# Other experts for the block ahead, the f32 form and the last group, with loads put ahead of the gathers and statistics behind

## The chip, the cores and the metric

The kernel runs on one core of a Trainium2 chip. The core has five engines that work side by side, each through its own list of instructions in order: TensorE (PE, matrix products), VectorE (DVE), ScalarE (ACT), GpSimd (POOL) and SyncE (SP, which here issues transfers). They meet by semaphores: an instruction may wait until another engine has counted something off, and all behind it on its engine wait too. The metric is the time of one execution in microseconds (us), median of several runs.

## The reference

```python
x = attention(q, k, v)                      # 4 batches, 8 heads, 576 tokens, 64 wide, causal by blocks of 64
x = elu(x @ w_in) @ w_out                   # 2304 tokens, 512 -> 2048 -> 512
do_compute = x @ w_skip > 0                 # the other tokens stay as they are
xc = x[do_compute]
e_idx = argmax(xc @ w_gate)                 # one of 8 experts for each token
gate_w = softmax(xc @ w_gate)[e_idx]
for e in range(8):                          # w1: 512 -> 1024, w2: 1024 -> 512
    y[e_idx == e] = gate_w * (relu(xc[e_idx == e] @ w1[e]) @ w2[e])
out[do_compute] = xc + y
```

With the inputs that are timed, experts 0 to 7 get 176, 2, 5, 91, 283, 192, 453 and 14 tokens.

## The kernel before

Attention, the dense layers and the choice of experts take the first 600 us or so. They are one stream of recorded instructions: `Recorder` notes each instruction with an estimated duration and what it reads and writes, and `order` puts them into a list for each engine. It goes by the earliest time at which an instruction can start by these estimates (`ready` sets a floor for it), takes steps marked `urgent` first, and lets other steps in where they end before the next urgent one would start. The lists are fixed when the kernel is built.

The experts follow. **Preparing an expert.** Its weights come in eight pieces of 512 KB (`load_w`), four for w1 (half 0) and four for w2 (half 1). For each half a statistic of every piece is taken (`stat_w`: the sum of squares on ACT, named jk, or the largest magnitude on DVE), a scale is worked out from it (`scale_w`, with a one-column matmul ns on PE), and each piece is then split into two f16 parts (`split_p`: one part by ACT, the other by DVE). A product of two f32 numbers becomes three f16 products. Experts in `PLAIN` aren't prepared: their blocks multiply in f32.

**A block** (`block`) works on 128 tokens, or on 64 where it is the first of an expert in `SMALL`. The tokens are gathered by POOL (an indirect transfer into gp) and transposed by a transfer that SP issues, into mxt or mxwo. PE makes hp in four groups of 24 matmuls; for each group ACT takes the relu (r) and the f16 part of it (hh), DVE the rest of it (hh); PE makes y from these; ACT scales y into o; POOL scatters o, added to the output. An f32 block has one record of PE for each pass over the weights, 64 for hp and 32 for y with 64 tokens.

**Order of the experts.** Blocks in `AHEAD` run before the counts of all experts are known, amid the end of the routing (their tiles are ahp, hha and ya). Then the experts in `ORDER` follow. Each has a first block in straight code (`first_tokens`) and then nested branches, one for each further 128 tokens (`more_tokens`); the innermost that isn't taken leads back to common code. Expert 2 has no straight block here, only the branches. Each of these places is scheduled by itself. The four experts of `LAST` have one straight stretch of four blocks, and a branch for further tokens.

**What is prepared beside what** stands in `PREP`: "6:l5-1 l3-0 c4-1 p4-1 s5-0|s5-1 c5-0 p5-0|..." means that beside expert 6's first block half 1 of expert 5 and half 0 of 3 are loaded (l), half 1 of 4 gets its scale (c) and is split (p) and half 0 of 5 gets its statistics (s); beside its next block what stands after the bar. `split_beside` records these steps behind the block's own; loads get the floor 5.0 us, statistics 2.0. A loaded piece needs a free place; a split gives the raw piece's place back. If a branch isn't taken, its share of the preparation stands in the other arm.

In what follows 6.0 is the first block of expert 6 behind the blocks ahead, 6.1 the next one. The blocks that run in this kernel are: ahead, expert 0 with 128 and expert 2 with 64 tokens; 6.0 to 6.3 with 128; 4.0 with 64, 4.1 and 4.2 with 128; 5.0 with 64, 5.1 with 128; and in the last group 0 with 64, 3 with 128, 1 and 7 with 64 in f32.

Of the kernel before, what the change touches and what calls it, by code (L numbers as in the profile page):

```python
# [24 lines left out]
PLAIN = 1, 7  # L25
EARLY = 0, 2, 6

SMALL = 0, 1, 4, 5, 7
# [319 lines left out]
def tile_kernel(ctx, tc, q, k, v, w_in, w_out, w_skip, w_gate, w1, w2, out):  # L348
# [34 lines left out]
    pm = const.tile([128, 4], F32)  # L383
# [40 lines left out]
    def setup_consts():  # L424
# [8 lines left out]
        for e in (2,) + SMALL:  # L433
            nc.vector.memset(carry[:, e:e + 1], 64.0)
        nc.gpsimd.iota(pm[:, 2:3], pattern=[[0, 1]], base=64, channel_multiplier=1, allow_small_or_imprecise_dtypes=True)
# [633 lines left out]
    AHEAD = [(0, 128), (2, 64)]  # L1069
    AH = {}  # L1070

    def ahead_gather():
# [13 lines left out]
        for i, (e, T) in enumerate(AHEAD):  # L1086
# [3 lines left out]
            rank = pm[:, 2:3] if T == 128 else pm[:, 0:1]  # L1090
            rc.gpsimd.tensor_scalar(out=a[:, 2:3], in0=rank, scalar1=carry[:, e:e + 1], scalar2=2 * BIG, op0=ALU.is_ge, op1=ALU.mult)

            rc.gpsimd.tensor_scalar(out=carry[:, e:e + 1], in0=carry[:, e:e + 1], scalar1=64.0 + T, scalar2=None, op0=ALU.max)
# [375 lines left out]
    def scale_w(e, which):  # L1469
# [11 lines left out]
        rc.tensor.matmul(out=p2, lhsT=ones16, rhs=cb, start=True, stop=True)  # L1481
        rc.vector.tensor_copy(acc[:, 5:6], p2)
# [16 lines left out]
    def prep_steps(e, which):  # L1499
        P_ = functools.partial  # L1500
        return ([("stat", P_(stat_w, e, which, x)) for x in range(4)] + [("scale", P_(scale_w, e, which))]
                + [("split", P_(split_p, e, 4 * which + x)) for x in range(4)])
# [22 lines left out]
    load_half(4, 0)  # L1525
    load_half(4, 1)
# [16 lines left out]
    io = mo.tile([128, 8 * NS], F32, tag="g", bufs=GB, name="io")  # L1543
# [46 lines left out]
    def fac_w(e):  # L1590
# [105 lines left out]
    def pre_gather(e):  # L1696
# [11 lines left out]
    def split_beside(e, part, at=5.0):  # L1708
        for h in sum(aside_of(e, part), []):
            if h[0] == "l":  # L1710
                load_half(int(h[1]), int(h[3]), at)
                continue
            for kind, f in prep_steps(int(h[1]), int(h[3])):
                if kind[1] == {"s": "t", "c": "c", "p": "p"}[h[0]]:
# [3 lines left out]
                    if h[0] == "s":  # L1718
                        rc.ready[len(rc.steps) - 1] = 2.0
# [10 lines left out]
    def first_tokens(e, fs):  # L1730
# [3 lines left out]
        rc.urgent = True  # L1734
        tokens(e, 0, place_of(e, 0), fs)
# [6 lines left out]
    def last_tokens(fs):  # L1742
# [19 lines left out]
    def more_tokens(e, j, fs):  # L1762
# [4 lines left out]
        with tc.If(cnt[e] > 128 * j, preferred_fallthrough_block=True, label=f"n{e}_{j}") as cmp:  # L1767
            if j < TM // 128:
# [4 lines left out]
                for x in {0: (0, 1, 2), 1: (1, 2, 3) if e in LAST else (3,)}.get(j, ()):  # L1773
# [42 lines left out]
    pre_gather(ORDER[1])  # L1816
# [57 lines left out]
    for h in "s4-0 s4-1 c4-0 p4-0 l5-0".split():  # L1874
# [8 lines left out]
    pre_gather(ORDER[2])  # L1883
# [43 lines left out]
```

## Time and profile before

| | us |
|---|---|
| median of three runs | 784.36 |
| lowest, highest | 783.33, 787.3 |
| the profiled execution | 785.88 |
| its span, first to last instruction | 784.0 |
| PE busy | 700.9 (89%) |
| DVE busy | 570.4 (73%) |
| ACT busy | 511.3 (65%) |

Times in the trace count from the start of the span; what the profiled execution took beyond it is 1.88 us. A busy share is an average over the whole span, in which the stages differ. For a list that is fixed, the question at each place is which engine stands, and what released it. The rows below are in the stretch from 600 us to the end. In a timeline row a bracket says how long the engine had been idle before, and what ended that; "ACTq" is ACT's sequencer, the part that handles branches and counts, and "PEld" is the loading of weights.

### The profile page before, as it was taken

What the parts mean: (1) busy time and instruction counts of PE and PEld (TensorE: products, weight loads), DVE (VectorE), ACT (ScalarE), POOL (GpSimd) and SP (SyncE); (2) the same over time, 40 slices, a digit from 0 to 9 for tenths busy, and PEclk for the clock granted to TensorE, in tenths of its full rate; (3) what the DMA queues carried; (4) which work ended last, traced back from release to release, by engine and by line L of the source; (5) the groups of instructions that cost most, each with busy time, mean ns of one, the idle gap of its engine ahead of it and who ended that gap; (6) DMA issues with size and microseconds to landing.
All of it is one profiled execution on the core that took longest, in us unless ns stands there. A gap on an engine that the chain in (4) does not pass through costs nothing. (4 is left out here: it accounts for less than half of the span.)

```text
span 784.0 us, 18160 instructions
## 1 busy us (share of the span) xinstructions
PE 700.9 (89%) x6766; PEld 466.2 (59%) x6766; DVE 570.4 (73%) x1710; ACT 511.3 (65%) x1132; POOL 92.0 (12%) x182
## 2 busy tenths in 40 slices
PE   4689997999998999989999999999999779869894
PEld 2467534764465655556656667675766656637673
DVE  5987999788997987978689648997777637143200
ACT  5966558989986886877587537673666667544310
POOL 2000000110001100101000100101040431313211
PEclk8579999999999999999999999999999898979998
DMA  9999899886979899999186189271546794492960
GB/s 263 298 257 281 258 255 199 168 134 125 183 146 139 146 197 180 157 184 179 38 145 125 32 173 382 74 224 42 182 106 185 151 269 109 80 273 46 292 158 5
DMA packets 279742, 134.03 MB, mean 171 GB/s; under 512 B 249291, under 2 KB 258005, under 8 KB 279120
## 3 DMA queue, kind: packets, MB, share of 16 engines
q1 hardware_dynamic: 275520, 125.42, 70.4%
q0 software_dynamic: 4112, 7.23, 4.6%
q8 instruction: 58, 0.95, 0.5%
q14 instruction: 52, 0.43, 0.2%
HBM read 74.12 MB, written 12.75 MB: 111 GB/s over the span
## 5 line engine op out<-in xcount | busy, mean ns | idle before, releaser
L310 PE MATMUL h<-xt,win 128*128 128x256 f16 x1344 | 158.1, 273 | 1.0 <-DVE n L310 1.0
L310 PE MATMUL y<-wout,g 128*128 128x512 f16 x672 | 157.4, 382 | 0.2 <-DVE g L310 0.2
L310 PEld LDWEIGHTS <-win 128*128 128x128 f16 x1344 | 127.6, 98 | 25.4 <-issue 3.1
L310 PEld LDWEIGHTS <-g 128*128 128x128 f16 x672 | 62.7, 98 | 70.8 <-issue 4.5
L310 ACT ACTIVATE ehl<-e,su 128x64 f16<-128x64 f32 (+4 forms) x208 | 85.7, 470 | 17.6 <-DMA et<-ehl 5.5
L310 ACT ACTIVATE e<-s,mx 128x64 f32<-128x64 f32 (+7 forms) x160 | 78.4, 493 | 25.3 <-DVE mx L310 10.5
L310 DVE SCALAR_TENSOR_TENSOR ehl<-e,su,ehl 128x64 f16<-128x64 f32 (+4 forms) x208 | 84.8, 441 | 6.9 <-ACT ehl L310 6.7
L310 DVE TENSOR_REDUCE mx<-s 128x1 f32<-128x64 f32 (+7 forms) x160 | 70.6, 449 | 13.5 <-PE s L310 12.8
L310 PE MATMUL s<-kt,qt 128*64 128x512 f16 (+7 forms) x640 | 62.8, 305 | 8.4 <-ACT e L310 5.5
L310 PE MATMUL xps<-et,vt 128*64 128x128 f16 (+1 forms) x1440 | 50.4, 219 | 16.2 <-DMA et<-ehl 9.9
L310 PEld LDWEIGHTS <-vt 128*64 128x64 f16 x1440 | 42.0, 115 | 35.5 <-issue 20.1
L310 PE MATMUL h<-xt,twi 128*128 128x256 f32 x256 | 62.1, 394 | 1.1 <-DVE g L310 1.1
L310 PE MATMUL y<-two,g 128*128 128x512 f32 x128 | 61.1, 610 | 0.0
L310 POOL MEMSET ehl<- 128x128 f16 x80 | 16.6, 213 | 357.4 <-DMA et<-ehl 275.6
L310 ACT ACTIVATE el<-h,col 128x512 f32<-128x512 f32 x56 | 38.2, 683 | 29.4 <-PE h L310 28.8
L310 PEld LDWEIGHTS h<-xt,twi 128*128 128x128 f32 x256 | 48.2, 195 | 10.9 <-DVE g L310 1.9
L310 PEld LDWEIGHTS <-qt 128*64 128x64 f16 x640 | 28.1, 114 | 43.2 <-issue 33.7
L310 PE MATMUL y<-p,hh 128*128 128x512 f16 (+1 forms) x222 | 41.0, 359 | 13.1 <-ACT hh L310 11.3
L310 ACT ACTIVATE g<-el,col 128x512 f16<-128x512 f32 x56 | 40.2, 717 | 18.9 <-DVE el L310 17.9
L310 PEld LDWEIGHTS <-hh 128*128 128x128 f16 (+1 forms) x336 | 26.4, 106 | 41.7 <-ACT hh L310 14.3
L1496 DVE SCALAR_TENSOR_TENSOR p<-p,n,p 128x1024 f16<-128x1024 f32 x30 | 38.3, 1281 | 12.3 <-ACT p L1495 12.2
L310 DVE TENSOR_TENSOR hh<-r,hh 128x256 f16<-128x256 f32 x38 | 15.9, 423 | 41.0 <-ACT hh L310 41.0
(231 smaller groups left out, 1185.5 us busy)
## 6 DMA issues: line engine op xcount, KB each, us to landing
p<-in_moe_w_dram SPq DMA_DIRECT2D x46, 512.0 KB, 7.1
rw<-in_moe_w_in_dram SPq DMA_DIRECT2D x16, 512.0 KB, 6.7
rw<-in_moe_w_out_dram SPq DMA_DIRECT2D x16, 512.0 KB, 5.0
pb<-in_moe_w_dram SPq DMA_DIRECT2D x13, 512.0 KB, 3.6
vflat<-in_v_dram SPq DMA_DIRECT2D x4, 1152.0 KB, 7.3
out_dram<-pay SPq DMA_DIRECT2D x18, 256.0 KB, 2.5
pay_d<-pay SPq DMA_DIRECT2D x18, 256.0 KB, 2.9
raw<-in_k_dram SPq DMA_DIRECT2D x16, 256.0 KB
```

The costliest lines, as they stand in the source:

```text
L310: rec.call(e, time, lambda: getattr(self.real, op)(*args, **kw), reads, writes, dma)
L1496: rc.call("dve", 1.2, lambda: nc.vector.scalar_tensor_tensor(out=half(1), in0=raw.t, scalar=sc, in1=half(0), op0=ALU.mult, op1=ALU.subtrac ...
```

## The change

Experts get other parts. The f32 form goes to expert 3 (128 tokens) instead of 1 and 7. The experts that are prepared ahead of everything are 0, 6 and 4 (before 0, 2 and 6). The second block ahead takes 128 tokens of expert 6 instead of 64 of expert 2. Expert 0's rest goes into `ORDER`, where its first block is straight code; expert 2 moves into `LAST`, and has blocks of 64 tokens as the first. Seven experts are prepared in place of six.

The steps beside the blocks get another order. Loads marked l are recorded ahead of the block and of its gathers, without a floor (`load_beside`); those marked m behind, as before. A statistic has the floor 4.0 instead of 2.0 and the scale's matmul the floor 3.0. `PREP` gives each block another share. In `last_tokens` the factors that combine two scales are recorded too, and loads and splits of expert 7 stand beside its blocks. The iota that the routing needs moves into another place in memory.

The blocks that then run are: ahead, 0 and 6 with 128 each; 0.0 with 64; 6.0 to 6.2 with 128; 4 and 5 as before; and in the last group 1 and 2 with 64, 3 with 128 in f32, 7 with 64.

```diff
-PLAIN = 1, 7
-EARLY = 0, 2, 6
-
-SMALL = 0, 1, 4, 5, 7
+PLAIN = 3,
+EARLY = 0, 6, 4
+
+SMALL = 0, 1, 2, 4, 5, 7
...
-    AHEAD = [(0, 128), (2, 64)]
+    AHEAD = [(0, 128), (6, 128)]
...
-            if T == 128:
+            if T == 128 and e not in SMALL:
+                rc.sync.dma_start(out=a[:, 0:2], in_=src[:, 0, :])
...
-    def scale_w(e, which):
+    def scale_w(e, which, wait=0.0):
...
+        if wait:
+            rc.ready[len(rc.steps) - 1] = wait
...
-    load_half(4, 0)
-    load_half(4, 1)
+    load_half(5, 0)
+    load_half(5, 1)
...
-    ORDER = [2, 6, 4, 5]
-    LAST = [0, 3, 1, 7]
-    XP = {2: 0, 6: 1, 4: 2, 5: 0}
+    ORDER = [0, 6, 4, 5]
+    LAST = [1, 2, 3, 7]
+    XP = {0: 1, 6: 2, 4: 0, 5: 1}
...
-    GATHERS = {6: [(6, 2), (5, 0), (5, 1)], 4: [(4, 2), (0, 0), (3, 0)], 5: [(5, 2), (1, 0), (7, 0)]}
+    GATHERS = {0: [], 6: [(6, 2), (4, 0), (4, 1)], 4: [(4, 2), (5, 0), (5, 1), (1, 0), (2, 0)], 5: [(5, 2), (3, 0), (7, 0)]}
...
     PREP = {int(e): [x.split() for x in h.split("|")] for e, h in (y.split(":") for y in (
-        "6:l5-1 l3-0 c4-1 p4-1 s5-0|s5-1 c5-0 p5-0|c5-1 p5-1,4:l3-1 l1-0 s3-0|c3-0 p3-0 s3-1,5:l1-1 l7-0 c3-1 p3-1,7:l7-1").split(","))}
+        "6:l1-1 m2-0 c5-0 p5-0|c5-1 p5-1 s1-0|s1-1 c1-0 p1-0,4:l2-1 m7-0|c1-1 p1-1 s2-0|s2-1 c2-0 p2-0,"
+        "5:l7-1 m3-0 c2-1 p2-1|s7-0 s7-1,8:l3-1 c7-0 p7-0 c7-1 p7-1").split(","))}
...
-    def split_beside(e, part, at=5.0):
+    def load_beside(e, part):
         for h in sum(aside_of(e, part), []):
             if h[0] == "l":
-                load_half(int(h[1]), int(h[3]), at)
+                load_half(int(h[1]), int(h[3]))
+
+    def split_beside(e, part):
+        for h in sum(aside_of(e, part), []):
+            if h[0] == "m":
+                load_half(int(h[1]), int(h[3]), 5.0)
+            if h[0] in "lm":
                 continue
-            for kind, f in prep_steps(int(h[1]), int(h[3])):
+            for kind, f in prep_steps(int(h[1]), int(h[3]), 3.0):
...
-                        rc.ready[len(rc.steps) - 1] = 2.0
+                        rc.ready[len(rc.steps) - 1] = 4.0
...
+        load_beside(e, 0)
         tokens(e, 0, place_of(e, 0), fs)
...
-    def last_tokens(fs):
+    def last_tokens():
 
         rc.begin()
         rc.late = rc.left
-        split_beside(LAST[-1], 0, 0.0)
+        load_beside(8, 0)
+        split_beside(8, 0)
         rc.urgent = True
+        fs = {e: fac_w(e) for e in LAST}
...
-    pre_gather(ORDER[1])
+    gather_to(0, 0)
+    pre_gather(6)
...
-    for h in "s4-0 s4-1 c4-0 p4-0 l5-0".split():
+    for h in "s5-0 s5-1 l1-0".split():
...
-            if e != 2:
+            if i:
                 hint(e, 1, cnt[e])
-                first_tokens(e, fs)
+            first_tokens(e, fs)
+            if i:
                 read_count(ORDER[i + 1] if i + 1 < len(ORDER) else "last")
             n0 = ng[0]
-            more_tokens(e, 0 if e == 2 else 1, fs)
+            more_tokens(e, 1, fs)
             ng[0] = n0
             FREE.extend(WHL.pop(8 * e + x) for x in range(8))
-        fs = {e: fac_w(e) for e in LAST}
         tc.mark_branch_hint_location("last", cnt["last"] > 128, engines=[mybir.EngineType.PE])```

SP's list from the start of expert 4's straight block, of before (the mx tiles are transposed tokens, p, pb and pd places for weights):

```order
L310 DMA_TRANSPOSE mxwo_1509<-gp_1505 128x8x128
L310 DMA_TRANSPOSE mxt_1507<-gp_1506 128x8x128
L310 DMA_TRANSPOSE mxt_1507<-gp_1505 128x8x128
L1450 DMA p_1475<-in_moe_w_dram 128x2x512
L1450 DMA p_7513<-in_moe_w_dram 128x2x512
L1450 DMA p_7528<-in_moe_w_dram 128x2x512
L1450 DMA p_7520<-in_moe_w_dram 128x2x512
L1447 DMA p_7521<-in_moe_w_dram 128x1024
```

and of after:

```order
L1453 DMA pd_1498<-in_moe_w_dram 128x2x512
L1453 DMA pd_1499<-in_moe_w_dram 128x2x512
L1453 DMA p_1476<-in_moe_w_dram 128x2x512
L1453 DMA p_7512<-in_moe_w_dram 128x2x512
L310 DMA_TRANSPOSE mxwo_1509<-gp_1501 128x8x128
L310 DMA_TRANSPOSE mxt_1507<-gp_1501 128x8x128
L310 DMA_TRANSPOSE mxt_1507<-gp_1502 128x8x128
L1450 DMA p_7513<-in_moe_w_dram 128x1024
L1450 DMA p_7514<-in_moe_w_dram 128x1024
```

Four loads stand ahead of the transposes now, and four behind; before all eight stood behind.

ACT's list in block 4.1 of before, from the relu of the first group of hp (jk is a statistic, p is a place being split):

```order
L310 ACTIVATE r_11455<-hp 128x256
L310 ACTIVATE hh<-r_11455 128x256
L1465 ACTIVATE jk,n_88<-p_1475 128x1024
L310 ACTIVATE r_11458<-hp 128x256
L1495 ACTIVATE p_7525<-p_7514,n_88 128x1024
L310 ACTIVATE hh<-r_11458 128x256
L310 ACTIVATE r_11461<-hp 128x256
L1495 ACTIVATE p_7526<-p_7515,n_88 128x1024
L310 ACTIVATE hh<-r_11461 128x256
```

and ACT's list at the end of block 4.2 of after, the last block of expert 4 that runs:

```order
L1468 ACTIVATE jk,n_87<-pd_1498 128x1024
L310 ACTIVATE r_11608<-hp 128x256
L310 ACTIVATE r_11611<-hp 128x256
L310 ACTIVATE hh<-r_11608 128x256
L310 ACTIVATE hh<-r_11611 128x256
L1468 ACTIVATE jk,n_87<-pd_1499 128x1024
L1500 ACTIVATE p_7528<-p_7530,n_87 128x1024
L1500 ACTIVATE p_7529<-p_7531,n_87 128x1024
L310 ACTIVATE o_1510<-y_11600,lists 128x512
L1500 ACTIVATE p_7530<-p_7532,n_87 128x1024
L1500 ACTIVATE p_7531<-p_7533,n_87 128x1024
L1782 COMPARE_AND_BRANCH
```

In before the statistic reads p_1475, the first of the loads that stand behind the transposes in the straight block of the same expert, and three groups of hh stand behind it; block 4.2 has no preparation at all. In after the statistic in 4.2 reads pd_1498, the first load in SP's list of after, and two splits stand between o and the branch.

## Rows read from the trace of the kernel before

**Rows 1.** The page's head, and its dense f32 groups (busy us, mean ns).
```profile
span 784.0 us, 18160 instructions
...
L310 PE MATMUL h<-xt,twi 128*128 128x256 f32 x256 | 62.1, 394 | 1.1 <-DVE g L310 1.1
L310 PE MATMUL y<-two,g 128*128 128x512 f32 x128 | 61.1, 610 | 0.0
```

**Rows 2.** PE's waits, 560 to 784: who is waited for, total, times, longest.
```profile
PE y L310 <- ACT hh L310: 12.6, 4, 7.1
PE hp L310 <- ACTq L1767: 5.7, 4, 3.0
PE ns L310 <- DVE cb L310: 2.0, 2, 1.1
```

**Rows 3.** PE's timeline: start, duration, tile, count, idle time before.
```profile
615.79 0.79 PE L310 MATMUL lp<-mv 128*128 128x152 f32 x4
619.55 1.79 PE L310 MATMUL hp<-mxt,p 128*128 128x128 f16 x24 [2.98 <-ACTq L1767]
622.48 0.16 PE L310 MATMUL ns<-cb,ones 128*128 128x1 bf16 x1 [1.14 <-DVE cb L310]
...
628.86 5.34 PE L310 MATMUL y<-p,hh 128*128 128x512 f16 x24
...
643.39 1.76 PE L310 MATMUL y<-p,hh 128*128 128x512 f16 x6 [2.79 <-ACT hh L310]
...
663.54 5.52 PE L310 MATMUL hp<-mxwo,p 128*128 128x128 f16 x96
668.90 5.34 PE L310 MATMUL y<-p,hh 128*128 128x512 f16 x24
...
696.53 1.03 PE L310 MATMUL y<-p,hh 128*128 128x512 f16 x2 [7.14 <-ACT hh L310]
...
715.21 0.33 PE L310 MATMUL hp<-mxt,pb 128*128 128x64 f16 x6 [0.89 <-ACTq L1767]
...
721.17 0.51 PE L310 MATMUL hp<-mxt,pb 128*128 128x128 f16 x6
...
734.12 4.44 PE L310 MATMUL hp<-mxt,p 128*128 128x64 f16 x120 [0.90 <-ACTq L1767]
...
752.02 7.25 PE L310 MATMUL hp<-x,p 128*128 128x64 f32 x64
```

**Rows 4.** ACT's timeline: splits before the branch, a statistic, the last o.
```profile
617.28 2.17 ACT L1495 ACTIVATE pd<-pb,n 128x1024 f16<-128x1024 f32 x2
...
693.72 1.06 ACT L1465 ACTIVATE jk<-p 128x1024 bf16<-128x1024 f32 x1 [8.62 <-DMA p<-in_moe_w_dram]
...
773.87 0.47 ACT L310 ACTIVATE o<-y,gp 128x256 f32<-128x256 f32 x1 [3.28 <-PEq L1753]
```

**Rows 5.** SP's timeline at expert 4: the first loads.
```profile
688.80 2.15 SPq L1450 DMA_DIRECT2D p<-in_moe_w_dram  x4
```

**Rows 6.** By window: busy PE, PEld, DVE, ACT, POOL, then PEclk, DMA share, GB/s.
```profile
621.00:627.00 6.00, 4.86 (x48) 4.70 (x46) 2.43 (x13) 3.56 (x7) 0.00 (x0) 0.50 0.69 112
...
693.00:702.00 9.00, 5.15 (x12) 1.62 (x13) 5.79 (x7) 8.06 (x14) 0.00 (x0) 0.50 1.04 398
702.00:774.00 72.00, 67.69 (x848) 53.40 (x846) 17.21 (x41) 22.28 (x48) 15.87 (x11) 1.00 0.56 140
```

**Rows 7.** Groups by line and shape, 600 to 784: busy us, mean ns.
```profile
L310 ACT ACTIVATE r<-hp 128x256 f32<-128x256 f32 x42 | 15.8, 379 | 33.9 <-PE hp L310 30.2 <-DVE pd L1496 2.0 <-remote 0.7
L310 ACT ACTIVATE hh<-r 128x256 f16<-128x256 f32 x38 | 15.5, 412 | 0.7
...
L1465 ACT ACTIVATE jk<-p 128x1024 bf16<-128x1024 f32 x8 | 8.4, 1051 | 10.5 <-DMA p<-in_moe_w_dram 10.4
...
L1496 DVE SCALAR_TENSOR_TENSOR p<-p,n,p 128x1024 f16<-128x1024 f32 x6 | 7.7, 1282 | 10.7 <-ACT p L1495 10.6
...
L1495 ACT ACTIVATE p<-p,n 128x1024 f16<-128x1024 f32 x6 | 6.9, 1144 | 0.3 <-DVE pb L1496 0.3
```

More of the change, by code (lines that the diff above doesn't have):

```diff
@@ L432, in setup_consts @@
         nc.vector.memset(carry, 0.0)
-        for e in (2,) + SMALL:
+        for e in SMALL:
             nc.vector.memset(carry[:, e:e + 1], 64.0)
+        nc.gpsimd.iota(pm[:, 4:5], pattern=[[0, 1]], base=0, channel_multiplier=1, allow_small_or_imprecise_dtypes=True)
         nc.gpsimd.iota(pm[:, 2:3], pattern=[[0, 1]], base=64, channel_multiplier=1, allow_small_or_imprecise_dtypes=True)
@@ L1089, in ahead_gather @@
             gp = gp2[:, 512 * i:512 * i + 512]
[L1090 removed]
+            rank = pm[:, 0:1] if T == 64 else pm[:, 2:3] if e in SMALL else pm[:, 4:5]
             rc.gpsimd.tensor_scalar(out=a[:, 2:3], in0=rank, scalar1=carry[:, e:e + 1], scalar2=2 * BIG, op0=ALU.is_ge, op1=ALU.mult)
[L1093 removed]
+            rc.gpsimd.tensor_scalar(out=carry[:, e:e + 1], in0=carry[:, e:e + 1], scalar1=64.0 * (e in SMALL) + T, scalar2=None, op0=ALU.max)
             rc.gpsimd.tensor_scalar(out=ai[:, 3:4], in0=a[:, 0:1], scalar1=2048.0, scalar2=float((AC + 1) * CT - 1), op0=ALU.add, op1=ALU.min)
@@ L1497, in split_p, with prep_steps @@
                 [raw.key, sc, hl.key], [hl.key])
-    def prep_steps(e, which):
+    def prep_steps(e, which, wait=0.0):
         P_ = functools.partial
-        return ([("stat", P_(stat_w, e, which, x)) for x in range(4)] + [("scale", P_(scale_w, e, which))]
+        return ([("stat", P_(stat_w, e, which, x)) for x in range(4)] + [("scale", P_(scale_w, e, which, wait))]
                 + [("split", P_(split_p, e, 4 * which + x)) for x in range(4)])
@@ L1542, in tile_kernel @@
     sl = part(NS)
-    io = mo.tile([128, 8 * NS], F32, tag="g", bufs=GB, name="io")
+    GP = []
+    for i in range(2):
+        t = wp.tile([128, 2, PW], F32, tag=f"wo{i + 4}", bufs=1, name=f"gp{i}")
+        GP += [t[:, 0, :], t[:, 1, :]]
+    more = GP.pop()
+    io = more[:, 352:352 + 8 * NS]
     rc.sync.dma_start(out=lst, in_=lst_d.rearrange("(e p s) w -> p e s w", e=E, p=128))
@@ L1596, in fac_w @@
         hs = half[:, e, C0[e], 1:2]
-        nc.vector.tensor_tensor(out=f, in0=nrm[e][:, 0, 7:8], in1=nrm[e][:, 1, 7:8], op=ALU.mult)
-        nc.vector.tensor_scalar(out=fs, in0=fs, scalar1=f, scalar2=2.0 ** 20, op0=ALU.mult, op1=ALU.mult)
+        rc.vector.tensor_tensor(out=f, in0=nrm[e][:, 0, 7:8], in1=nrm[e][:, 1, 7:8], op=ALU.mult)
+        rc.vector.tensor_scalar(out=fs, in0=fs, scalar1=f, scalar2=2.0 ** 20, op0=ALU.mult, op1=ALU.mult)
         if e in SMALL:
-            nc.vector.tensor_scalar(out=hs, in0=hs, scalar1=f, scalar2=2.0 ** 20, op0=ALU.mult, op1=ALU.mult)
+            rc.vector.tensor_scalar(out=hs, in0=hs, scalar1=f, scalar2=2.0 ** 20, op0=ALU.mult, op1=ALU.mult)
         return fs
@@ L1772, in more_tokens @@
                 rc.urgent = True
-                for x in {0: (0, 1, 2), 1: (1, 2, 3) if e in LAST else (3,)}.get(j, ()):
+                for x in ((1, 2, 3) if e in LAST or e == 0 else (3,)) if j == 1 else ():
                     gather_to(e, x)
```

15 lines of the change are left out of this document (5 added, 10 removed).

## The prediction, made before the changed kernel ran

> **What bounds the kernel now.** I read the page's head first, for the span and the busy shares, then PE's waits from 560 us on, then PE's timeline there, and at each wait the timeline of the engine that ended it. The order of PE is the same up to 600 us; only the experts' stretch behind it is changed, so all that follows is there.
>
> PE is busy for most of that stretch, and where it stands, ACT ended it: 12.6 us in four waits of y for hh, 5.7 us in four waits for ACT's sequencer at branches, 2.0 us in two waits of ns for the scale [rows 2]. The largest, 7.14 us at 696.53 [rows 3], isn't ACT being slow. ACT stood 8.62 us before a statistic at 693.72, and a transfer ended that [rows 4]: the load had been issued at 688.80 only [rows 5], behind three transposes in SP's list, and the groups of hh that y needs stand behind the statistic in ACT's list. The wait of 2.79 us at 643.39 is of the same kind (its statistic stood before a load too). The wait of 2.98 us before 619.55 is another kind: PE's last matmul ended at 616.6 (615.79 + 0.79), ACT's last split at 617.28 + 2.17 = 619.45, and PE goes on 0.1 us later [rows 3, 4]. PE waits at a branch until ACT has done its whole list of that place. Three other such places cost (5.7 - 3.0) / 3 = 0.9 us each [rows 2].
>
> Each long stall has a second price. The granted clock is 0.50, the lower of the two levels (1.2 GHz), from 621 to 627 and from 693 to 702, behind the stalls of 2.98 and 7.14 us, and 1.00 from 702 to 774 although PE stood 0.9 us there twice [rows 3, 6]. From 619.55 to 628.86 the 96 matmuls hp and one wait of 1.14 us took 9.31 us; 96 at the higher clock take 668.90 - 663.54 = 5.36 [rows 3]. So the low clock cost 9.31 - 5.36 - 1.14 = 2.8 us.
>
> **The sum, part by part.** I follow PE, the engine that the end hangs on, and build its new timeline from blocks. A clean block of 128 tokens takes 10.7 us (663.54 to 668.90 + 5.34), one of 64 tokens 721.17 - 715.21 = 6.0 us [rows 3].
>
> *The blocks ahead.* 128 tokens of expert 6 instead of 64 of expert 2: 10.7 - 6.0 = 4.7 us more. PE ended at 616.6 here, so now at 621.3; a little earlier if the longer list fills gaps of the routing. The branch of the empty expert 2, with its 2.98 us, goes, since expert 0's block follows in straight code. Block 0.0 (6.0) and an ordinary branch (0.9): 628.2.
>
> *Expert 6* has three blocks instead of four, which removes 10.7 us. Two costs are new. The statistics and scale of one half and the splits of another now stand beside each of 6.1 and 6.2, where before the last block was clean. ACT's work in 6.1 is four r (0.38), four hh (0.41), four statistics (1.05, with the read-out of the sum about 1.2), four splits (1.14) and o (about 0.7) [rows 7]: 3.2 + 4.8 + 4.6 + 0.7 = 13.3 us against PE's 10.7. So ACT runs late into 6.2, the scale of 6.2 is late, and ns waits; I take 0.8, by the two waits of ns that sum to 2.0 [rows 2]. And behind o two splits still stand before the branch, as the order of 4.2 shows too. The stall of 2.98 us had just this form, o and two splits; with one wait for DVE's part of a split (1.28, [rows 7]) it would be 4.3. I take 3.5, between 0.9 (ACT gets done in time) and 4.3. Expert 6: 3 x 10.7 + 0.8 + 3.5 = 36.4, to 664.6.
>
> *Expert 4* is 4.0, 4.1, 4.2 as before. Removed are the wait of 7.14 us in 4.1 and one of about 1.3 in 4.0 (12.6 less 7.14 and 2.79 leaves 2.7 for two): the pieces whose statistics stand in 4.1 are now loaded beside 6.0, and those of 4.2 by the four loads at the head of SP's list in 4.0. New are the same two costs as at expert 6, and in 4.0 both r stand ahead of both hh, which makes the first hh one r late (with a wait about 0.7). 6.0 + 0.7 + 10.7 + 10.7 + 0.8 + 3.5 = 32.4, to 697.0.
>
> *Expert 5.* Its block 5.1 has eight statistics, the last ones behind o: I take 2.3 us at the branch, two of them, between 0.9 and 3.5. 6.0 + 0.7 + 10.7 + 2.3 = 19.7, to 716.7.
>
> *The last group* took 773.87 - 734.12 = 39.7 us [rows 3, 4]. Now it has three blocks of 64 in f16, 18.0 us, and 128 tokens of expert 3 in f32. The trace has no such block. Its 64 records of hp cost 7.25 us with 64 columns [rows 3], the lower end, and 64 x 62.1 / 256 = 15.5 with 256 columns [rows 1], the upper. Half of the price at 256 columns for half the columns is 7.8, close to the lower end; I take that. Its y has 16 records of 512 columns, 16 x 61.1 / 128 = 7.6 [rows 1]. 18.0 + 7.8 + 7.6 = 33.4, to 750.1. Beside it stand eight splits of expert 7 on ACT (9.2 us) and DVE (10.2), in 27 us before they are needed, and four loads that are due 20 us later: nothing.
>
> The Trainium skill bears on that f32 price. Its page "TensorE: Matmul & The Clock Gate", section "Weight-path perf modes — Fast Weight Load (FWL) and DoubleRow", says that the fast way to load weights is not used for FP32, so that at few columns the loading sets the price. By that rule hp would stay near 7.25, by half of the row of 256 columns it is 7.8; no run here has yet shown 128.
>
> *The end.* From PE's last work to the end of the span is 784.0 - 773.9 = 10.1 us, the last scatter, unchanged: 760.2.
>
> *The clock.* The two stalls of 3.5 us are longer than the 2.98 and 2.79 that had low clock behind them. Twice 2.8: 765.8. The seventh expert's preparation (eight more splits and statistics) is what fills ACT in these places and is priced there; it isn't added again.
>
> On this the Trainium skill (same page, "Loop structure matters more than you think") says that a long wait between bursts of matmuls lets the array fall to the lower clock, which speaks against putting work behind o. The rows at 619.55 and 696.53 agree. By that rule both exits are paid twice; without it the sum would be 5.6 us lower.
>
> The profiled execution took 785.88 with a span of 784.0, so 1.88 lies around it, and it is 1.52 above the median of 784.36. A span of 765.8 gives 765.8 + 1.88 - 1.52 = 766.2. I say 766.
>
> **Rivals.**
>
> *The exits are short.* ACT has finished by PE's end at all three branches (0.9 each instead of 3.5, 3.5 and 2.3, 6.6 less) and the clock stays at 1.00 (5.6 less): 754. For it: ACT is idle in long pieces in 4.2 and 6.3 of before, and lists by estimates can fit. Against: the order puts the splits behind o. Chance 0.14.
>
> *A statistic still waits for a load.* If a load finds no free place in time (the first places of 4.0 come free by splits in 6.2, which are late), one stall like 7.14 with its clock returns: 766 + 7.1 + 2.8 = 776. For it: the loads at 4.0 and 5.0 are only a block or two ahead. Against: before, the load was issued in the very block in which the statistic stood, and 5 us passed from 688.80 to 693.72 [rows 4, 5]; now a block of 6 us at least lies between. Chance 0.14.
>
> *The loads hold back the transposes* (the other side). At 0.0, 4.0, 5.0 and the last group four loads of 512 KB now stand before the transposes; at the 398 GB/s of 693 to 702 [rows 6] 2.1 MB take 5.3 us. If transposes come that late to a block, PE stands 5.3 us and pays 2.8 for the clock, 8.1 a place. With three such places it is 766 + 24 = 790, slower; with two it is 782. For it: SP works in order. Against: what is gathered at 4.0 is used in 4.2 and by expert 5, at least 16 us later. Chance 0.03.
>
> *The change doesn't gain what it moves.* The seventh expert's preparation takes ACT six statistics and eight splits more, 6 x 1.05 + 8 x 1.14 = 15.4 us [rows 7]. If ACT bounded all of the stretch, that would come on top: 781, about no change. Against: ACT stood 10.4 us for transfers before statistics of p places alone [rows 7], time that it can now work in. Chance 0.06.
>
> **How the numbers follow.** The forecast has 0.63 and by itself reaches from 761 (one exit short, clock kept there) to 773 (hp in f32 at the upper end). With the first two rivals 754 to 778 holds 0.85 or somewhat more. What a measurement of this kernel can tell from no change is 0.5%, 3.9 us: faster is below 780.4, slower above 788.3. Faster: 0.63 + 0.14 + 0.14 = 0.91. About the same: 0.05, nearly all of the last rival. Slower: 0.04, the transposes and a part of the last rival.
>
> **What would show it.** Right: no wait of y for hh above 1.5 us behind a statistic that a transfer released; PE's first hp of block 0.0 near 621; waits for ACT's sequencer of some 3.5 us at the ends of 6.2 and 4.2 with the granted clock at 0.50 behind them; the f32 block of expert 3 near 15 us. Wrong: a statistic that still stands for a transfer (the second rival), branches of 0.9 us (the first), waits of hp for a transfer of mxwo or mxt (the third), or PE standing for hh in block after block (the fourth).

## The result, and the profile after

The changed kernel takes 759.03 us (median of four runs, 756.81 to 760.74), the kernel before 785.36 on the same occasions. The ratio is 0.966, with a 95% interval of 0.963 to 0.970. The forecast was 766, with 754 to 778 as its range. The profiled execution took 760.74 with a span of 758.9. Executions that took over 1.5% more than the fastest of their kernel are left out of the ratios below (one each in experiments 2, 3 and 5), and in 2 and 3 it is the profiled one.

PE's waits from 560 us on, of the changed kernel (who is waited for: total, times, longest), answer to [rows 2]:

```profile
PE hp L310 <- ACTq L1782: 9.5, 4, 3.2
PE y L310 <- ACT hh L310: 1.7, 2, 0.8
PE hp L310 <- issue: 1.4, 2, 0.7
PE ns L310 <- DVE cb L310: 0.4, 2, 0.2
```

The waits of y for hh are down from 12.6 us to 1.7, and the waits at branches are up from 5.7 to 9.5. PE's timeline shows where these are (start, duration, what, count, and idle time before it with what ended it):

```profile
616.77 0.68 PE L310 MATMUL lp<-mv 128*128 128x152 f32 x4
617.29 2.96 PE L310 MATMUL hp<-mxt,p 128*128 128x64 f16 x96
620.18 2.81 PE L310 MATMUL y<-p,hh 128*64 128x256 f16 x48
624.14 4.19 PE L310 MATMUL hp<-mxwo,p 128*128 128x128 f16 x72 [1.14 <-ACTq L1782]
...
659.55 4.51 PE L310 MATMUL hp<-mxt,p 128*128 128x64 f16 x96 [3.20 <-ACTq L1782]
664.89 3.05 PE L310 MATMUL y<-p,hh 128*64 128x256 f16 x48 [0.83 <-ACT hh L310]
...
692.74 0.42 PE L310 MATMUL hp<-mxt,p 128*128 128x64 f16 x9 [3.20 <-ACTq L1782]
...
714.48 0.42 PE L310 MATMUL hp<-mxwo,pb 128*128 128x64 f16 x9 [1.97 <-ACTq L1782]
...
728.75 7.41 PE L310 MATMUL hp<-x,p 128*128 128x128 f32 x64
736.00 7.03 PE L310 MATMUL y<-p,r 128*128 128x512 f32 x16
```

From 624.14 to the end of the last y of expert 6, 3.20 us before 659.55, PE never stands longer than 0.2 us, through three blocks. Expert 0's block follows the routing (616.77 + 0.68) at once. The three long waits are at the branches that end experts 6, 4 and 5; I call them exits. ACT's timeline at the first of these, with o and the two splits behind it, and one statistic of 4.1:

```profile
656.40 0.69 ACT L310 ACTIVATE o<-y,lists 128x512 f32<-128x512 f32 x1 [0.72 <-PE y L310]
656.98 1.14 ACT L1500 ACTIVATE pb<-pd,n 128x1024 f16<-128x1024 f32 x1
658.31 1.15 ACT L1500 ACTIVATE pd<-pd,n 128x1024 f16<-128x1024 f32 x1 [0.19 <-DVE pb L1501]
...
672.39 1.05 ACT L1468 ACTIVATE jk<-p 128x1024 bf16<-128x1024 f32 x1
```

The last split ends at 659.46 and PE goes on at 659.55. The statistic at 672.39 has no idle time before it; the one in the same block before stood 8.62 us for its load [rows 4]. In the windows behind the exits (busy PE, PEld, DVE, ACT, POOL, then the granted clock, the transfers' share and GB/s) the clock is near the lower level, as in [rows 6]:

```profile
660.00:664.00 4.00, 4.00 (x87) 3.94 (x83) 1.29 (x4) 0.39 (x1) 0.00 (x0) 0.57 0.74 139
664.00:668.00 4.00, 3.12 (x53) 2.59 (x51) 1.45 (x6) 1.00 (x4) 3.11 (x3) 1.00 0.85 243
...
694.50:698.00 3.50, 3.44 (x64) 3.35 (x63) 1.02 (x7) 0.38 (x1) 0.00 (x0) 0.53 1.18 262
...
714.50:718.00 3.50, 3.50 (x72) 3.50 (x72) 0.90 (x8) 0.80 (x2) 0.71 (x1) 0.55 0.93 284
```

### The profile page after: what moved, and what is told of

The parts are those of the page before. It is cut to its first block, busy times and chain, and to the rows that moved or that the text cites. A ratio compares the mean times of both kernels' runs of the same rounds, so it can differ in the third digit from the quotient of the medians.

```text
span 758.9 us, 18318 instructions
## 1 busy us (share of the span) xinstructions
PE 686.4 (90%) x6824; PEld 461.8 (61%) x6824; DVE 583.2 (77%) x1736; ACT 523.8 (69%) x1148; POOL 98.9 (13%) x183
## 5 line engine op out<-in xcount | busy, mean ns | idle before, releaser
L310 PE MATMUL h<-xt,win 128*128 128x256 f16 x1344 | 158.1, 273 | 1.0 <-DVE n L310 1.0
L310 PE MATMUL y<-wout,g 128*128 128x512 f16 x672 | 156.0, 380 | 0.0
L310 PEld LDWEIGHTS <-win 128*128 128x128 f16 x1344 | 127.6, 98 | 25.4 <-issue 3.1
L310 PEld LDWEIGHTS <-g 128*128 128x128 f16 x672 | 62.5, 98 | 69.7 <-issue 3.4
L310 ACT ACTIVATE ehl<-e,su 128x64 f16<-128x64 f32 (+4 forms) x208 | 85.7, 471 | 17.2 <-DMA et<-ehl 5.5
L310 ACT ACTIVATE e<-s,mx 128x64 f32<-128x64 f32 (+7 forms) x160 | 78.6, 494 | 24.3 <-DVE mx L310 10.8
L310 DVE SCALAR_TENSOR_TENSOR ehl<-e,su,ehl 128x64 f16<-128x64 f32 (+4 forms) x208 | 84.8, 440 | 5.7 <-ACT ehl L310 5.4
L310 DVE TENSOR_REDUCE mx<-s 128x1 f32<-128x64 f32 (+7 forms) x160 | 70.5, 448 | 14.8 <-PE s L310 14.2
L310 PE MATMUL s<-kt,qt 128*64 128x512 f16 (+7 forms) x640 | 62.9, 306 | 7.6 <-ACT e L310 4.1
L310 PE MATMUL h<-xt,twi 128*128 128x256 f32 x256 | 62.8, 396 | 1.4 <-DVE g L310 1.3
L310 PE MATMUL xps<-et,vt 128*64 128x128 f16 (+1 forms) x1440 | 50.5, 219 | 14.7 <-DMA et<-ehl 6.7
L310 POOL MEMSET ehl<- 128x128 f16 x80 | 16.8, 216 | 356.8 <-DMA et<-ehl 248.2
L310 PEld LDWEIGHTS <-vt 128*64 128x64 f16 x1440 | 42.1, 115 | 34.1 <-issue 20.0
L310 PE MATMUL y<-two,g 128*128 128x512 f32 x128 | 60.9, 609 | 0.0
L310 ACT ACTIVATE el<-h,col 128x512 f32<-128x512 f32 x56 | 38.3, 683 | 28.6 <-PE h L310 28.0
L310 PEld LDWEIGHTS h<-xt,twi 128*128 128x128 f32 x256 | 48.4, 195 | 11.6 <-DVE g L310 2.6
L310 PEld LDWEIGHTS <-p 128*128 128x128 f16 x936 | 46.9, 102 | 11.7 <-issue 6.7
L310 PEld LDWEIGHTS <-qt 128*64 128x64 f16 x640 | 28.2, 114 | 41.9 <-issue 31.8
L310 ACT ACTIVATE g<-el,col 128x512 f16<-128x512 f32 x56 | 40.2, 717 | 18.5 <-DVE el L310 17.5
L310 DVE SCALAR_TENSOR_TENSOR g<-el,col,g 128x512 f16<-128x512 f32 x56 | 41.6, 743 | 3.7 <-ACT g L310 3.6
L1501 DVE SCALAR_TENSOR_TENSOR p<-p,n,p 128x1024 f16<-128x1024 f32 x32 | 40.8, 1280 | 3.1 <-ACT p L1500 3.0
L310 DVE SCALAR_TENSOR_TENSOR el<-h,col,el 128x512 f32<-128x512 f32 x56 | 41.7, 744 | 1.2
```

The lines of the kernel that those rows point to most:

```text
L310: rec.call(e, time, lambda: getattr(self.real, op)(*args, **kw), reads, writes, dma)
L1501: rc.call("dve", 1.2, lambda: nc.vector.scalar_tensor_tensor(out=half(1), in0=raw.t, scalar=sc, in1=half(0), op0=ALU.mult, op1=ALU.subtrac ...
```

## The experiments

Times are medians; each ratio is to the kernel before in the same runs, since that differed from one set of runs to the next (782.7 to 786.0). Single executions of one kernel lie up to 13 us apart, so differences under 3 us are not told apart here. Lengths of stages come from one profiled execution each, and are measured from PE's own rows. In those of the changed kernel and of experiments 2 to 12 the first hp of block 0.0 starts anywhere from 613.9 to 622.9 us, with the same instructions ahead of it, so stages are compared by their lengths and not by their ends.

**1. The kernel before, with loads first and statistics later.**

```diff
+    def load_beside(e, part):
+        for h in sum(aside_of(e, part), []):
+            if h[0] == "l":
+                load_half(int(h[1]), int(h[3]))
...
-            for kind, f in prep_steps(int(h[1]), int(h[3])):
+            for kind, f in prep_steps(int(h[1]), int(h[3]), 3.0):
...
-                        rc.ready[len(rc.steps) - 1] = 2.0
+                        rc.ready[len(rc.steps) - 1] = 4.0
...
+        load_beside(e, 0)
         tokens(e, 0, place_of(e, 0), fs)
```

Three of the loads are marked m, and stay behind the block.

> The kernel before with its own experts, its own blocks and its own shares of the preparation, but with the order of the steps of the changed kernel: the loads marked l ahead of the block, statistics with the floor 4.0 and the scale with 3.0. My theory: in the kernel before, what was lost at 6.1 (2.79 + 1.34 + 0.25 us) and 4.1 (7.14 + 0.32 us) was lost to loads issued late, and the low clock behind them cost 2 x 2.8 us; this order alone removes most of that, about 17 us, and leaves the stall at expert 2's empty branch: 767 to 773. Rival 1, the gain lies in which experts are placed where and the order alone brings nothing: 783 to 787. Rival 2, the later floors only move the stalls to the branches: one of the two gains is given back, 774 to 780.

769.79 us, ratio 0.980 (0.975 to 0.984), as my theory has it. The order alone is worth some 16 of the 26 us. ACT's statistics of p places waited 10.4 us for transfers before [rows 7] and 0.9 here, and the wait at the empty branch of expert 2 is still there:

```profile
PE hp L310 <- ACTq L1777: 5.7, 4, 3.0
PE y L310 <- ACT hh L310: 3.8, 2, 2.1
```

**2. The changed kernel with loads and statistics in the order of before.**

```diff
-                load_half(int(h[1]), int(h[3]))
+                pass
...
-            if h[0] == "m":
-                load_half(int(h[1]), int(h[3]), 5.0)
+            if h[0] in "lm":
+                load_half(int(h[1]), int(h[3]), 0.0 if e == 8 else 5.0)
...
-            for kind, f in prep_steps(int(h[1]), int(h[3]), 3.0):
+            for kind, f in prep_steps(int(h[1]), int(h[3])):
...
-                        rc.ready[len(rc.steps) - 1] = 4.0
+                        rc.ready[len(rc.steps) - 1] = 2.0
```

> The changed kernel with its experts and shares, but the steps in the order of before: all loads recorded behind the block and its gathers with the floor 5.0 (0.0 in the last group), statistics with the floor 2.0, the scale without one. My theory: the shares already put each statistic one block or more behind its load, so only the late statistics of 5.1 can wait, and with early statistics ACT ends with o in 6.2 and 4.2, so two exits of 3.2 us fall to about 1: 752 to 762 against 759 for the changed kernel. Rival, loads first is what removed the stalls: they return at two places, 7 + 2.8 us each, 772 to 780.

772.66 us, ratio 0.981 (0.976 to 0.986). My theory falls, the rival holds: the shares of the preparation don't protect the statistics by themselves. In 4.2 a statistic of DVE stood 6.21 us for the last of the loads that are recorded in 4.0, which SP issued at 685.87 only, when PE was in 4.2; hh stood behind it, and y for hh:

```profile
697.35 3.17 PE L310 MATMUL y<-p,hh 128*128 128x512 f16 x7 [4.34 <-DVE hh L310]
```

```profile
695.74 1.22 DVE L1470 TENSOR_REDUCE n<-p 128x1 f32<-128x1024 f32 x1 [6.21 <-DMA p<-in_moe_w_dram]
```

This execution took 778.23 us; how much the five shorter ones lost there isn't shown. By the ratios the experts' arrangement alone gives some 15 us, the order alone 16, both 26: a little less than a sum, by a difference that lies within the intervals. No run takes the arrangement's part to pieces. By the rows, the wait of 2.98 us at expert 2's empty branch is gone, and the last group is shorter (39.7 us before, 34.1 after).

**3. Early statistics, loads first.**

```diff
-            for kind, f in prep_steps(int(h[1]), int(h[3]), 3.0):
+            for kind, f in prep_steps(int(h[1]), int(h[3])):
...
-                        rc.ready[len(rc.steps) - 1] = 4.0
+                        rc.ready[len(rc.steps) - 1] = 2.0
```

> The changed kernel with loads first, but statistics with the floor 2.0 and the scale without one, as in before. In ACT's lists of 6.2 and 4.2 o is now the last step. My theory: the branches at the ends of 6 and 4 fall from 3.2 us to about 1 and the low clock behind them goes (about 1.6 us each), while hh waits some tenths more in the blocks: 751 to 757. Rival, the later statistics keep hh from waiting: with early ones y waits for hh in four blocks by 1 us or more each and the kernel is at 761 to 768.

766.74 us, ratio 0.975 (0.970 to 0.980). The exits did what I expected (0.9, 1.2 and 0.96 us), and yet it is slower than the changed kernel. The rival gives the right time and the wrong reason: y waited for hh 1.0 us in all. What came instead is of two kinds. PE waited 3.0 us for the scale in 6.2 and 4.2 (0.4 in the changed kernel), since the edit drops the floor of the scale's matmul too. And there are 7.9 us of waits of hp (1.4 in the changed kernel) that the profile puts to "issue", nothing that it shows, in the middle of a run of matmuls. PE's timeline behind the branch of 5.1:

```profile
720.23 0.42 PE L310 MATMUL hp<-mxwo,pb 128*128 128x64 f16 x9 [0.96 <-ACTq L1782]
...
720.84 0.19 PE L310 MATMUL hp<-mxwo,pd 128*128 128x64 f16 x1
724.42 0.27 PE L310 MATMUL hp<-mxwo,pd 128*128 128x64 f16 x2 [3.39 <-issue]
...
730.59 0.31 PE L310 MATMUL hp<-mxwo,p 128*128 128x64 f16 x5
733.40 1.80 PE L310 MATMUL hp<-mxwo,p 128*128 128x64 f16 x33 [2.50 <-issue]
```

The queues in the first of these stalls, 721 to 724.4 (packets, MB, share of the 16 engines' time), and the windows of the stall and behind it:

```profile
q1 hardware_dynamic: 562, 1.24, 109.2%
q0 software_dynamic: 13, 0.03, 4.2%
q8 instruction: 1, 0.02, 1.8%
q14 instruction: 1, 0.01, 0.6%
```

```profile
721.00:724.40 3.40, 0.03 (x2) 0.00 (x0) 0.14 (x3) 0.00 (x0) 0.86 (x1) 0.84 1.16 378
724.40:728.00 3.60, 3.58 (x68) 3.57 (x68) 0.69 (x3) 0.80 (x2) 0.00 (x0) 0.50 1.21 129
```

The weight loads fill the engines at 378 GB/s, and one packet each of the instruction queues is among them. That made a second theory: PE waits for its own instructions, which are fetched by transfers behind 2 MB of weights. In the changed kernel it stands at the branch for ACT meanwhile. The sizes are those of one execution, of 773.67 us, 13 us above the profiled one of the changed kernel; 5.6 of these 13 us had passed before block 0.0 (622.88 against 617.29).

**4. Late statistics, loads behind.** The loads' edit of experiment 2 alone.

> The changed kernel with its late statistics, but all loads recorded behind the block and its gathers, with the floor 5.0 (0.0 in the last group), as in before. My theory: the statistics stand a block or more behind their loads anyway, so it costs 0 to 4 us, most of it at the statistics of 5.1: 758 to 764. Rival, loads first is what removed the stalls: 770 to 780.

765.09 us, ratio 0.976 (0.971 to 0.980), a little over my range. In 5.1 two statistics of ACT stood 1.2 and 2.0 us for loads, and the exits of 4 and 5 grew from 3.2 and 2.0 us to 4.15 and 5.4: what is late behind o comes out at the branch.

```profile
PE hp L310 <- ACTq L1782: 13.5, 4, 5.4
```

**5. Spare matmuls at the exits.**

```diff
                 rc.issue()
+                if (e, j) in ((6, 2), (4, 2), (5, 1)):
+                    spare = misc([128, 512], "spare", "pv")
+                    wt = WHL[8 * e + 4].t.bitcast(F16).rearrange("p (a f) -> p a f", a=2)
+                    for i in range(7 if e == 5 else 12):
+                        rc.tensor.matmul(out=spare, lhsT=place_of(e, j)[:, 0, :], rhs=wt[:, 0, 0:512], ...)
```

> The changed kernel with spare matmuls on PE at the end of blocks 6.2 and 4.2 (12 of 128x512 in f16 each, 2.6 us) and of 5.1 (7, 1.5 us), into a tile that nothing reads, in the time in which PE waits at the branch for ACT (3.2, 3.2 and 2.0 us). They leave PE's waits where they are and keep PE busy through them. My theory: the low clock behind the three exits (659.6 to 664, 694.5 to 698, 714.5 to 718) comes from PE standing, costs 1.6 us or so each, and goes: 753 to 757 against 759. Rival, the clock falls there for another reason, or the spare work delays the branch by as much: 758 to 762.

760.44 us, ratio 0.963 (0.959 to 0.967) against 0.966 (0.963 to 0.970): not told apart. Two of six executions had a mean clock of 0.99 and took 753.7 and 754.3 us, the others 0.96 and 758.9 to 765.4. In the profiled one, of the second kind, PE then stood for "issue" three times:

```profile
PE hp L310 <- issue: 3.9, 2, 2.6
PE hp L310 <- ACTq L1782: 3.3, 4, 0.9
PE y L310 <- issue: 2.2, 1, 2.2
```

PE went on 0.3 to 0.4 us later than without the spare matmuls (3.5, 3.5 and 2.4 us from the end of y to the next hp). Two executions are too few to price the clock by; what is shown is that work in place of the wait doesn't shorten the median.

**6 and 7. The preparation moved, so that the exits are short.**

```diff
-6:l1-1 m2-0 c5-0 p5-0|c5-1 p5-1 s1-0|s1-1 c1-0 p1-0,4:l2-1 m7-0|...|s2-1 c2-0 p2-0,5:l7-1 m3-0 c2-1 p2-1|s7-0 s7-1,8:l3-1 ...
+6:l1-1 m2-0 c5-0 p5-0|c5-1 p5-1 s1-0|s1-1,4:c1-0 p1-0 m2-1 m7-0|...|s2-1,5:c2-0 p2-0 m7-1 m3-0|c2-1 p2-1 s7-0,8:l3-1 s7-1 ...
```

In the seventh run s7-0 moves to the last group as well.

> The changed kernel with other shares: the scale and splits of 1-0 go from 6.2 to 4.0, those of 2-0 from 4.2 to 5.0, those of 2-1 from 5.0 to 5.1, the statistics of 7-1 from 5.1 to the last group; the loads 2-1 and 7-1 then stand behind the block. o is then the last step of ACT in 6.2 and 4.2. My theory: the exits of 6 and 4 fall from 3.2 us to about 1, that is 4.5 us and the low clock behind them (3 us), less about 1 us of waits in the short blocks 4.0 and 5.0: 750 to 756. Rival, as in the runs with early statistics PE then stands for its own instructions behind the branches ('issue' in its waits, beside four weight loads in flight), and the time behind a branch is lost anyway: 758 to 765.

> The run with the preparation moved, and the statistics of 7-0 moved from 5.1 to the last group too, so that o is ACT's last step in 5.1 but for nothing. My theory: the exit of 5.1 falls from about 2 us to about 1 as well: 0 to 2 us less than the run before it, unless the last group then waits for expert 7's splits. Rival: the wait turns into 'issue' behind the branch, no difference, or expert 7's block waits for its scale and it is 2 to 6 us slower.

762.78 us (ratio 0.971, 0.969 to 0.974) and 765.6 (0.974, 0.972 to 0.977). The exits of 6 and 4 fell to 0.9 us in both, and that of 5 in the seventh run, whose median is nevertheless the higher one. Both theories of mine fall. The rivals have the times right, and the reasons in part: in experiment 6 PE stood 2.3 us for "issue", but 2.9 us for the scale that now stands in 5.0, and the exit of 5 grew from 2.0 to 3.9 us. In the seventh PE stood 5.0 us for "issue", 2.8 us for the same scale, and in the last group 1.6 us for loads of expert 3.

**8. Early statistics, expert 3's w1 nearly not loaded.** On top of the edit of experiment 3:

```diff
-                nc.sync.dma_start(out=pl.t, in_=w1[e][p * 128:(p + 1) * 128, :])
+                n_ = 64 if e == 3 else 1024
+                nc.sync.dma_start(out=pl.t[:, 0:n_], in_=w1[e][p * 128:(p + 1) * 128, 0:n_])
```

> The changed kernel with statistics early (766.7 us), in which only 64 of 1024 columns of each piece of expert 3's w1 are loaded; what is left out is 15/16 of that transfer, so expert 3's products are of other numbers, and the work on the engines is the same. In that run PE stood 3.4 us at 721 behind the branch at the end of 5.1 for nothing that the profile shows, while these four loads were landing. Theory: PE waits there for its next instructions, which come by transfers too, behind the 2 MB of the loads: the stall falls to under 1 us and 3 to 6 us are gained with the low clock behind it, 761 to 764. Rival: the stall is the same without the loads: 766 to 768.

753.77 us, ratio 0.960 (0.956 to 0.964) against 0.975 for experiment 3. The gain, some 12 us by the ratios, is over what I expected. The same matmul now waits 0.35 us instead of 3.39, and the other one 0.42 instead of 2.50:

```profile
709.89 0.22 PE L310 MATMUL hp<-mxwo,pd 128*128 128x64 f16 x2 [0.35 <-issue]
...
714.20 1.41 PE L310 MATMUL hp<-mxwo,p 128*128 128x64 f16 x43 [0.42 <-issue]
```

So the stall hangs on these loads. What PE waited for while they landed isn't shown by that: a smaller load leaves room for everything else that moves there, not for instructions alone.

**9. The changed kernel with that small load.** The edit of experiment 8 on the changed kernel.

> The changed kernel itself with only 64 of 1024 columns of each piece of expert 3's w1 loaded (what is left out is 15/16 of that transfer, so expert 3's products are of other numbers). With early statistics this was worth 13 us (766.7 to 753.8), most of it in the last group (41.4 to 32.8 us). Theory: PE's own instructions wait behind those loads, and in the changed kernel they arrive while PE stands at the branch of 5.1 for ACT anyway; so here it is worth little, 1 to 4 us, 755 to 758. Rival: the loads cost the same wherever the branch wait ends, 8 us or more: 746 to 751.

758.95 us, ratio 0.970 (0.965 to 0.975): no gain. The same 2 MB cost some 12 us where PE stands at the branch of 5.1 for 1 us, and nothing that can be measured where it stands there 2 us for ACT.

**10 and 11. Half 0 of expert 3 loaded in the last group.** In the changed kernel, and with early statistics.

```diff
-5:l7-1 m3-0 c2-1 p2-1|s7-0 s7-1,8:l3-1 c7-0 ...
+5:l7-1 c2-1 p2-1|s7-0 s7-1,8:l3-0 m3-1 c7-0 ...
```

> The changed kernel with the load of half 0 of expert 3 moved from 5.0 to the head of the last group, half 1 behind it. Theory: the loads no longer land at the branch of 5.1 but beside the first two blocks of the last group, where PE fetches instructions too: stalls of 'issue' there grow from 1.4 us to 3 or 4, 760 to 765. Rival, the last group has room: 756 to 759.

> The changed kernel with statistics early (766.7 us) and half 0 of expert 3 loaded at the head of the last group. Theory: the stall of 3.4 us behind the branch of 5.1 goes with the loads that were landing there, but 2 MB land a few us later, beside the same blocks: 3 to 7 us are won of the 13 that the small load won, 759 to 764. Rival, the stall only moves: 765 to 770.

758.38 us (ratio 0.968, 0.964 to 0.972) and 757.33 (0.966, 0.963 to 0.970). Loading later costs nothing in the changed kernel (the rival). With early statistics it wins 7 us by the ratios (0.975 to 0.966), at the upper end of what I had thought; the time itself lies below my range since the kernel before was 3 us faster on that occasion. Where PE stands at the branch for 1 us, it pays to keep the load out of the few us behind it.

**12. Early statistics beside experts 6 and 4 alone.**

```diff
-            for kind, f in prep_steps(int(h[1]), int(h[3]), 3.0):
+            for kind, f in prep_steps(int(h[1]), int(h[3]), 0.0 if e in (6, 4) else 3.0):
...
-                        rc.ready[len(rc.steps) - 1] = 4.0
+                        rc.ready[len(rc.steps) - 1] = 2.0 if e in (6, 4) else 4.0
```

> The changed kernel with statistics early and scales without a floor in the branches of experts 6 and 4 alone; expert 5 and the last group as in the changed kernel, with its wait of 2 us at the branch of 5.1. Theory: in the run with early statistics and a small load, expert 6 took 34.5 us and expert 4 30.2 against 35.4 and 33.2 in the changed kernel, since the exits were 0.9 us instead of 3.2, and what it lost it lost behind 5.1; so this one gains 3 to 4 us: 754 to 757. Rival, what is saved at an exit comes back as 'issue' in the next expert's first block, as it did behind 5.1: 758 to 763.

756.0 us, ratio 0.964 (0.960 to 0.969). The time is as the theory has it, and the lowest median of all that compute the whole; by the ratio the gain is some 1.5 us, and it is not told apart from the changed kernel (0.966) nor from experiment 5 (0.963). In its profiled execution (751.83 us) expert 6 took 34.4 us and expert 4 30.0 (35.4 and 33.2 in the changed kernel), and PE stood at the last branch only for a transfer:

```profile
708.02 0.42 PE L310 MATMUL hp<-mxwo,pb 128*128 128x64 f16 x9 [2.14 <-DMA mxwo<-gp]
```

What stands at the branch of 5.1, how long the last group then takes (first hp to the end of the last y), and the whole of the experts (first hp of block 0.0 to the same end), side by side, each from one execution:

| run | wait at the branch, us | last group, us | all experts, us |
|---|---|---|---|
| changed kernel | 1.97 | 34.1 | 131.3 |
| 4, loads behind | 5.4 | 34.0 | 136.4 |
| 6, preparation moved | 3.9 | 33.8 | 132.3 |
| 9, small load | 1.96 | 31.9 | 126.5 |
| 10, load later | 1.96 | 33.2 | 131.6 |
| 12, early statistics in 6 and 4 | 2.14 (for a transfer) | 31.8 | 122.3 |
| 2, loads and statistics of before | 5.6 | 38.2 | 143.9 |
| 3, early statistics | 0.96 | 41.4 | 138.8 |
| 7, statistics in the last group | 0.88 | 41.4 | 133.6 |
| 5, spare matmuls | 0.89 | 37.0 | 135.0 |
| 8, early statistics, small load | 0.96 | 32.8 | 124.8 |
| 11, early statistics, load later | 0.96 | 33.0 | 126.0 |

A short wait goes with a long group, unless the loads are out of the way. A long wait goes with a short one, except in experiment 2, where y stood 3.1 us for "issue" later in the group. Of the 41.4 us of the seventh run about 3 are its own: 1.6 us for loads and 1.4 for hh.

Two things narrow down what a short wait changes. PE isn't through the branch earlier, counted from the four loads of half 0 of expert 3: it goes on 5.2 us behind the first of them in experiment 3 (issued at 715.02), 4.9 in 5 and 4.8 in the changed kernel (709.72). And in experiment 12 these loads were issued from 707.95 on, so that they landed behind the branch, at some 320 GB/s from 710 to 716, and no "issue" came. What 3 and 5 have in common is that PE stood idle there for 1 us only; in 5 it had the spare matmuls. This fits the second theory, if the fetch goes on while PE stands; it doesn't show it. At expert 4's exit it is alike: where PE stood there for 0.9 to 1.2 us (2, 3, 5 to 8, 11 and 12), 0.9 to 2.6 us of "issue" followed in block 5.0; where it stood 3.2 us or more (the changed kernel, 4, 9 and 10), 0.7 at most. The first of these lines is of the changed kernel, the second of experiment 5:

```profile
694.54 0.32 PE L310 MATMUL hp<-mxt,pb 128*128 128x64 f16 x3 [0.68 <-issue]
690.90 0.25 PE L310 MATMUL hp<-mxt,pb 128*128 128x64 f16 x3 [2.61 <-issue]
```

## Why the prediction was right, and where its sizes were off

The mechanism was right: loads issued before the blocks take away the waits of statistics, hence of hh and y; the price is ACT's list behind o at three branches; the low clock followed these in the profiled execution. What the sum did not say is what the later statistics are worth: with the loads first and the statistics early the kernel is some 7 us slower (experiment 3), as it is with the statistics late and the loads behind (4); where expert 3's load comes later too, early ones cost nothing (11). By the steps of the sum, on the timeline of the profiled execution:

| step | forecast, us | measured, us |
|---|---|---|
| block 0.0 starts | 621.3 | 617.3 |
| 0.0 and its branch | 6.9 | 6.85 |
| expert 6 with its exit | 36.4 | 35.4 |
| expert 4 with its exit, and low clock behind the one before | 32.4 + 2.8 | 33.2 |
| expert 5 with its exit, likewise | 19.7 + 2.8 | 21.7 |
| last group | 33.4 | 34.1 |
| the end, from PE's last work | 10.1 | 10.3 |

**The start of block 0.0** is the term that was mis-sized, 4 us of the 7 by which the forecast lies above the profiled span. I added 4.7 us for 128 tokens of expert 6 ahead. From the same group of ya (598.90 before, 597.82 after) to the end of the routing it takes 19.6 us instead of 17.7: PE's busy time there grew by 3.6 us (15.58 to 19.13) and not by 4.7, and its idle time fell from 2.1 us to 0.5. That gaps would fill I had named and not sized. The other 1.1 us stood before; 0.7 of it is there at 560 us already, where PE's list is still the same, and is chance: in the executions of the experiments that group of ya starts anywhere from 594.1 to 602.5.

**The exits** were 3.20, 3.20 and 1.97 us; the forecast 3.5, 3.5 and 2.3. The form of the first stall of before, o and two splits, was the right row to price them by.

**The scale in 6.2 and 4.2** waited 0.2 us, not 0.8: ACT does run late out of 6.1 (its o starts at 646.32, 0.9 us behind the end of PE's y), but the late floor puts ns behind 72 matmuls, and there it finds its input:

```profile
649.65 0.16 PE L310 MATMUL ns<-cb,ones 128*128 128x1 bf16 x1 [0.19 <-DVE cb L310]
```

Without the floor, in experiments 3, 8, 11 and 12, ns stands behind 24 matmuls and waits 1.5 us in 6.2 and in 4.2; here in 12:

```profile
648.08 0.17 PE L310 MATMUL ns<-cb,ones 128*128 128x1 bf16 x1 [1.49 <-DVE cb L310]
```

Early statistics with the floor of the scale kept, which these rows suggest, were not tried.

**The low clock** came behind all three exits, the one of 1.97 us too, which I had left out; but each cost less. The 96 matmuls of 64 columns took 4.51 us at 659.55 and 2.96 at 617.29, so some 1.6 us and not 2.8. That three times some 1.6 is nearly twice 2.8 is luck. Nor does such a wait always bring the low clock. The same 3.20 us before the same 96 matmuls, in experiments 9 and 10:

```profile
657.32 4.50 PE L310 MATMUL hp<-mxt,p 128*128 128x64 f16 x96 [3.20 <-ACTq L1783]
658.57 2.96 PE L310 MATMUL hp<-mxt,p 128*128 128x64 f16 x96 [3.20 <-ACTq L1782]
```

In 10 the granted clock was 1.00 from 658.5 to 662. In 9 it was 1.00 behind the other two exits, of 3.20 and 1.96 us (690.5 to 698 and 710 to 718). On the rule that I took from the Trainium skill ("TensorE: Matmul & The Clock Gate", "Loop structure matters more than you think"), that long waits lead to the lower clock, the three exits of the changed kernel's profiled execution agree; those of 9 and 10 show that 3.2 us don't always do it. So this term is paid in some executions and not in others.

**The f32 block** of expert 3: 7.25 us for hp (728.75 to 736.00), against 7.8 forecast, and 6.9 for y against 7.6. That hp costs the same with 128 columns as with 64 [rows 3] agrees with the Trainium skill (same page, "Weight-path perf modes — Fast Weight Load (FWL) and DoubleRow"): the loading of weights sets the price. From 728.7 to 736 the loading was busy 7.25 of 7.30 us; in the y behind it, of 512 columns, 3.08 of 7.00.

**The rivals.** No statistic of the experts' blocks waited for a load, no transpose held PE, and PE did not stand for hh block after block. Of the first rival, short exits and 754 us, the condition was made by hand: three short exits in experiments 3 and 7 (766.7 and 765.6 us), two in 6 (762.8), and in 5 the waits were filled with work (760.4). Its price is wrong: in 3, 5 and 7 the last group is 3 to 7 us longer, and in 6 and 7 the moved scale costs 2.8 to 2.9 us in 5.0. Where the loads are kept away (8, 11) the loss in the last group goes, and where the wait at the last branch stays (12) it doesn't come; of these only 8, which leaves out most of a load, stands out from the changed kernel (0.960 against 0.966, with intervals that just touch).

What stays open: that the stalls put to "issue" are PE's own instructions is inferred from the instruction packets in the stall, and from experiments 8, 9 and 11, which took the load away; the trace does not tie a packet to an engine. What a short wait at the branch changes is read from one execution of each run. And the clock and these stalls vary from one execution to the next, which the medians don't take apart.

## What to carry to other kernels

Where an engine that works in order stands for a transfer, look for when that transfer was issued and what stood before it in its queue: here the order of the steps alone was worth 16 us, without any work saved. Before shortening a wait, ask what else goes on during it: where a wait of 2 us at a branch was cut to 1, stalls of several us came behind it, by inference fetches that the wait had hidden. Matmuls added where the engine has gaps cost less than their length (here 1.9 us of a forecast 4.7), so size the gaps first. And before a wait is priced with a low clock behind it, look whether other executions of the same code have it.

## What the runs showed of the hardware

Where PE had stood for 0.96 us at a branch, it stalled for 3.39 us in the middle of a run of matmuls, with nothing waited for that the profile shows, while a load of 2 MB landed (experiment 3); with 1/16 of the load the same matmul stood 0.35 us (8). Where PE had stood for 2.14 us first, the same 2 MB landed behind the branch without such a stall (12). A wait of 1.97 us had the granted clock at 0.55 behind it in the changed kernel (714.5 to 718), and one of 1.96 us at the same place left it at 1.00 in experiment 9 (710 to 718). After 3.20 us it was 0.57 in one execution (660 to 664) and 1.00 in another (experiment 10, 658.5 to 662). Waits of 0.9 us before had left it at 1.00 [rows 6].
